# An attention and gated-MLP kernel on one core: 19 layer-norm statistics computed on ACT, k's column maxima of batches 2 to 7 by block transposes on DVE, and a new order of all steps

## The chip, the core and the metric

The kernel runs on one core of one Trainium2 chip. Its engines work side by side: PE (matrix products; PEld is its weight load), DVE (vector work), ACT (activation functions and copies), POOL (slower vector work) and SP (issues the transfers). The metric is the device time of the core in microseconds. Before the change three runs took 533.49, 533.83 and 534.16 us, a median of 533.83 us.

## What is computed

Attention with two softmaxes feeds a gated MLP whose gate mixes along the sequence. In the reference, cut to what matters (8 batches, 8 heads, 576 positions, 64 channels per head; x has 512 channels, the MLP 1024):

```python
q_s = softmax(q, axis=-1)            # over the 64 channels of a head, maximum subtracted
k_s = exp(k - np.max(k, axis=2, keepdims=True))
k_s = k_s / (np.sum(k_s, axis=2, keepdims=True) + 1e-09)     # over the 576 positions
kv = np.einsum('bhsd,bhse->bhde', k_s, v)
x = heads_joined(np.einsum('bhsd,bhde->bhse', q_s, kv))      # 8 x 576 x 512
h = gelu_tanh(x @ w_in)              # 1024 wide
u, v = h[..., :512], h[..., 512:]
v_n = (v - mean(v)) / np.sqrt(var(v) + 1e-06) * g_ln         # over the 512
v_s = np.einsum('ts,bsd->btd', w_sg, v_n) + b_sg[None, :, None]
return x + (u * v_s) @ w_out
```

## The kernel before

All of the kernel is a list of steps, the string `PLAN`. The loop at its end reads a step such as `hv_mm 3 1` and calls the function of that name with those numbers; a letter behind (`V`, `G`, `A`) names the engine of an elementwise operation that can go to several. The wrapper `InOrder` makes every engine issue its instructions in the order of `PLAN`, and matmuls are kept in that order too. Nothing reorders at run time: an instruction that waits holds all behind it on its own engine. All DVE, ACT and POOL instructions are issued on one line (L142 before), all matmuls on L330.

Precision: values that enter the large products are split into a rounded high part and a rest, and each product is three matmuls (high by high, rest by high, high by rest).

The steps of one batch b, in halves h of four heads, tiles i of 128 positions and quarters f, d, e of 128 channels:

- `load_q`, `load_k`, `load_v`: transfers on SP's queue.
- q's softmax: `q_max` (DVE), `q_swapm` (4 ACT copies of 32 rows), `q_top` (DVE), `q_sub` (POOL or DVE), `q_exp` (ACT), `q_sum` (DVE), `q_swapd` (4 ACT copies), `q_inv` (DVE), `q_mul` (POOL or DVE, twice), `q_turn` (DVE transpose, twice).
- k's softmax: `k_max` reduces five tiles to one of 128x256 in `km` by three DVE maxima. The maximum across the 128 partitions is then found by PE: `kt_mm` transposes `km` with the identity `eye` (two matmuls), `k_top` (DVE) reduces along the row to `kt`, `kb_mm` transposes `kt` back while repeating it to all partitions (two matmuls), `k_sub` (DVE, 128x1280, one operand in PSUM) subtracts it and `k_exp` (ACT) follows. `kv_mm` is 40 small matmuls; `kv_inv` and `kv_scale` (DVE) divide by the sums.
- `x_mm` gives x; `x_high` (ACT) and `x_low` (DVE) split it. `hv_mm` (12 matmuls of 512 columns) gives the v half of h, `hv_gelu` (ACT) its gelu, `hv_stat` (DVE: BN_STATS, BN_AGGREGATE and an addition of epsilon to `ve`) the statistics of a tile, `hv_pow` (POOL) the inverse root, `hv_norm` (DVE) subtracts the mean and multiplies by g_ln, `hv_high` (ACT) and `hv_low` (DVE) scale and split. The tail of 64 positions of two batches is one tile, `hv ... 4`, whose split is `tail_high`, `tail_low`, `tail_again`. That makes 36 tiles in all.
- `hu_mm` (24 matmuls of 288 columns) and `hu_gelu` give u; `sg_mm` (28 matmuls) the mixing along the sequence; `gate` (DVE) the product; `gate_high` (ACT), `gate_low` (DVE or POOL) its split; `out_mm` (24 matmuls), `out_add` (DVE), `out_rest` (DVE or POOL), `out_store` the result.
- Before that, w_in, w_out and w_sg are loaded and split once (`wi_a` to `wi_l`, `wo_a` to `wo_l`, `ws_h`, `ws_l`, `b_h`, `b_l`).

`x_mm`, `hu_mm`, `sg_mm` and `out_mm` share three PSUM buffers in turn (ps2), `hv_mm`, `kv_mm`, `kt_mm` and `kb_mm` two others (ps1). A matmul into a buffer waits until the reader of what stood in it three (or two) turns earlier is done: `hu_gelu`, `gate`, `out_add`, `x_low` for ps2, `hv_gelu`, `kv_scale`, `k_top`, `k_sub` for ps1.

## Time and profile before

| | before |
|---|---|
| median of three runs | 533.83 us (533.49 to 534.16) |
| profiled execution | 533.9 us, of which the span of the profile is 532.0 us |
| PE busy | 484.2 us (91%) in 3824 matmuls |
| DVE busy | 378.7 us (71%) in 646 instructions |
| ACT busy | 249.5 us (47%) in 425 instructions |
| POOL busy | 126.1 us (24%) in 104 instructions |
| clock granted to PE | 9 in tenths in every slice |

The profile is of one execution. Busy times are sums over the instructions of an engine; where matmuls overlap at their ends the overlap is counted once. 1.9 us of the execution lie outside the span.

### The profile page before, as it was taken

The page shows a single profiled execution, that of the slowest core. Times are in us where ns is not written, and L with a number is a line of the kernel's source. Part 1 is how long each engine was busy: PE and PEld are TensorE (multiplying, and loading weights), DVE is VectorE, ACT ScalarE, POOL GpSimd, SP SyncE. Part 2 cuts the span into 40 slices and gives each one's busy share as a digit, 9 for nine tenths or more (in the row PEclk, how much of TensorE's full clock was granted, in tenths as well). Part 3 has the DMA queues.
Part 4 walks back from the last instruction along what each step waited for, and adds up shares of the span by engine and source line. Part 5 has one row for each costly group of instructions (what it writes and reads, how often), then busy time and mean ns, then how long its engine had stood idle before and what let it go on. Part 6 is the DMA issues. An engine that isn't in the chain of part 4 may idle for free.

```text
span 532.0 us, 9264 instructions
## 1 busy us (share of the span) xinstructions
PE 484.2 (91%) x3824; PEld 444.3 (84%) x3824; DVE 378.7 (71%) x646; ACT 249.5 (47%) x425; POOL 126.1 (24%) x104
## 2 busy tenths in 40 slices
...
GB/s 322 369 388 96 17 217 81 1 46 121 168 90 38 253 91 2 44 101 68 130 39 101 111 123 90 1 101 123 67 1 1 68 23 0 1 1 68 23 1 90
DMA packets 19054, 48.87 MB, mean 92 GB/s; under 512 B 1602, under 2 KB 8132, under 8 KB 19012
## 3 DMA queue, kind: packets, MB, share of 16 engines
...
## 4 chain that ended last, share of the span: by engine, by line
PE 74%; DVE 17%; issue 3%; DMA 2%; ACT 2%; POOL 1%; SPq 0%; POOLq 0%; DVEq 0%; ACTq 0%
PE ps L330 74%; DVE km L142 2%; DVE ot_i L142 2%; DMA qq<-q 1%; DVE qm L142 1%; DVE qd L142 1%; DVE kk L142 1%; DVE v L142 1%; POOL qq L142 1%; DMA kk<-k 1%; DVE qq L142 1%; DVE s L142 1%; DVE x_l L142 1%; DVE wi_l L142 1%; DVE ulow L142 1%
## 5 line engine op out<-in xcount | busy, mean ns | idle before, releaser
L142 POOL TENSOR_TENSOR rs<-ve,half 128x1 f32<-128x1 f32 x36 | 31.0, 860 | 157.1 <-DVE ve L142 152.1
L142 DVE TENSOR_TENSOR u<-ps,u 128x576 f32<-128x576 f32 x32 | 24.0, 750 | 52.0 <-PE ps L330 52.0
L330 PE MATMUL ps<-ulow,wo_h 128*128 128x288 f32 x256 | 55.7, 296 | 1.2 <-DVE ulow L142 1.2
L330 PE MATMUL ps<-gh,wo_h 128*128 128x288 f32 x256 | 56.1, 298 | 0.5 <-ACT gh L142 0.5
L330 PE MATMUL ps<-ws_h,vnh 128*128 128x288 f32 x256 | 55.8, 299 | 0.0
L330 PE MATMUL ps<-gh,wo_l 128*128 128x288 f32 x256 | 55.3, 294 | 0.0
L330 PE MATMUL ps<-ws_l,vnh 128*128 128x288 f32 x256 | 54.8, 295 | 0.0
L330 PE MATMUL ps<-ws_h,vnl 128*128 128x288 f32 x256 | 54.8, 295 | 0.0
L142 ACT ACT_TABLE_LOAD x38 | 48.8, 1283 | 8.0 <-PE ps L330 5.1
L142 ACT ACTIVATE v<-ps 128x512 f32<-128x512 f32 x36 | 21.5, 598 | 63.8 <-PE ps L330 62.3
L142 ACT CAST gh<-u 128x576 fp32r<-128x576 f32 x32 | 21.5, 671 | 57.5 <-DVE u L142 57.3
L142 DVE TENSOR_TENSOR o<-ps,x_h 128x576 f32<-128x576 f32 (+1 forms) x33 | 24.2, 734 | 31.8 <-PE ps L330 31.8
L142 POOL TENSOR_TENSOR qq<-qq,qd 128x576 f32<-128x576 f32 x22 | 28.2, 1295 | 68.6 <-DVE qd L142 46.2
L330 PEld LDWEIGHTS ps<-gh,wo_h 128*128 128x128 f32 x256 | 41.4, 188 | 1.9 <-ACT gh L142 0.8
L142 POOL TENSOR_TENSOR ulow<-u,gh 128x576 fp32r<-128x576 f32 x16 | 23.8, 1487 | 80.7 <-ACT gh L142 62.9
L330 PEld LDWEIGHTS ps<-ulow,wo_h 128*128 128x128 f32 x256 | 41.2, 188 | 2.0 <-DVE ulow L142 1.9
L330 PEld LDWEIGHTS ps<-ws_h,vnh 128*128 128x128 f32 x256 | 41.3, 189 | 0.4
L330 PE MATMUL ps<-wi_h,x_h 128*128 128x512 f32 x144 | 40.7, 404 | 1.0 <-DVE kk L142 1.0
L330 PEld LDWEIGHTS ps<-ws_h,vnl 128*128 128x128 f32 x256 | 41.3, 188 | 0.0
L330 PEld LDWEIGHTS ps<-ws_l,vnh 128*128 128x128 f32 x256 | 41.3, 188 | 0.0
L330 PEld LDWEIGHTS ps<-gh,wo_l 128*128 128x128 f32 x256 | 41.2, 188 | 0.0
L330 PE MATMUL ps<-x_h,wi_h 128*128 128x288 f32 x256 | 40.8, 303 | 0.0
...
## 6 DMA issues: line engine op xcount, KB each, us to landing
...
```

The costliest lines, as they stand in the source:

```text
L142: ins = op(*args, **kw)
L330: tc.keep_in_program_order(nc.tensor.matmul(*args, **kw))
```

## The change

Three things are altered.

First, the statistics of 19 of the 36 tiles (0 2, 0 3, 0 4, 1 2, 2 0, 2 1, 2 4, 3 0 to 3 3, 4 2, 5 3, 6 0, 6 1, 6 3, 7 0, 7 2, 7 3) are computed on ACT. `hv_gelu` gets the letter `A` and writes the row sum beside its output; the new step `hv_sq` multiplies the sum by -1/512 (an ACT instruction on 128x1) and squares v minus the mean over 128x512 with the row sum of the squares as second output; `hv_stat ... A` is one DVE instruction on 128x1 in place of three.

Second, for batches 2 to 7 (`FOLD`) `kt_mm`, `k_top` and `kb_mm` are replaced by steps without PE: `k_fold` (DVE: a transpose of 32x32 blocks of 128x256, and a reduction to `kf`, 128x8), `k_rota` (4 ACT copies of 32x8, which move each group of 32 partitions by one), `k_maxa` (DVE, 128x8), `k_rotb` (4 ACT copies, by two), `k_maxb` (DVE: 128x8, and a block transpose that repeats the result over 128x256). `k_sub` then reads both operands from SBUF, and five of them (2 0, 4 0, 5 1, 6 1, 7 1) go to POOL.

Third, `PLAN` is written in another order from its first line to its last, the loads included, and other steps carry the letters: on DVE stand 6 instead of 8 `q_sub`, 8 instead of 10 `q_mul`, 22 instead of 16 `gate_low`, 13 instead of 20 `out_rest` and 2 instead of 4 `ws_l`; the others of these are on POOL. 50 instead of 38 loads of ACT's function tables follow from the order on ACT. The last steps, from `out_mm 7 2` on, read as before but for the quarter that each works on.

```diff
+FOLD = (2, 3, 4, 5, 6, 7)
 PLAN = """
...
-kt_mm 2 1, kb_mm 2 0, k_top 2 1, sg_mm 0 2, hv_pow 1 2, q_exp 2 0, gate 0 0, k_sub 2 0, hv_norm 1 2, gate_high 0 0, q_sum 2 0, k_exp 2 0
...
+k_maxa 3 1, q_inv 3 0, load_v 4 0, q_mul 3 0 1, q_mul 3 0 0, k_rotb 3 1, q_sum 3 1, sg_mm 1 1, hu_gelu 1 2, k_maxb 3 1, k_sub 3 1, q_swapd 3 1
+gate 1 2, k_exp 3 1, k_max 4 0, sg_mm 1 3, gate 1 1, k_fold 4 0, gate_high 1 1, q_inv 3 1, gate_high 1 2, gate_low 1 1, k_rota 4 0, kv_mm 3 1
...
+    kf_s, ka_s, kb_s = (slots(n, 2, [P, 8]) for n in ("kf", "ka", "kb"))
+    sq = sb("sq", [P, DV])
+    sm_s, nm_s, sv_s = (slots(n, 6, [P, 1]) for n in ("sm", "nm", "sv"))
...
+    def blocks(b, h, i):
+        return km_s(b, h)[:, i * 256:i * 256 + 256].rearrange("p (j c) -> p j c", c=32)
+
+    def k_fold(b, h):
+
+        m = km_s(b, h)
+        V.transpose(out=m[:, 256:512], in_=m[:, 0:256])
+        V.tensor_reduce(out=kf_s(b, h, at=h), in_=blocks(b, h, 1), axis=AX.X, op=ALU.max)
+
+    def rotate(dst, src, n):
+        for i in range(4):
+            j = (i + n) % 4
+            A.copy(out=dst[i * 32:i * 32 + 32], in_=src[j * 32:j * 32 + 32])
+
+    def k_rota(b, h):
+        rotate(ka_s(b, h, at=h), kf_s(b, h), 1)
+
+    def k_maxa(b, h):
+        V.tensor_tensor(out=kf_s(b, h), in0=kf_s(b, h), in1=ka_s(b, h), op=ALU.max)
+
+    def k_rotb(b, h):
+        rotate(kb_s(b, h, at=h), kf_s(b, h), 2)
+
+    def k_maxb(b, h):
+
+        f = kf_s(b, h)
+        V.tensor_tensor(out=f, in0=f, in1=kb_s(b, h), op=ALU.max)
+        V.transpose(out=blocks(b, h, 1), in_=f[:, :, None].broadcast_to([P, 8, 32]))
+
-    def k_sub(b, h):
+    def k_sub(b, h, E=V):
         kk = kk_s(b, h, at=h)
-        V.tensor_tensor(out=kk, in0=kk, in1=st["kb", b, h][:, None, 0:256].broadcast_to([P, 5, 256]), op=ALU.subtract)
+        top = km_s(b, h)[:, 256:512] if b in FOLD else st["kb", b, h][:, 0:256]
+        E.tensor_tensor(out=kk, in0=kk, in1=top[:, None].broadcast_to([P, 5, 256]), op=ALU.subtract)
...
+    def hv_sq(b, i):
+
+        A.mul(nm_s(b, i), sm_s(b, i), -1.0 / DV)
+        A.activation(sq, v_s(b, i), AF.Square, bias=nm_s(b, i), accum_out=sv_s(b, i))
+
+    def hv_stat(b, i, E=V):
+        if E is A:
+            V.tensor_scalar(out=ve_s(b, i), in0=sv_s(b, i), scalar1=1.0 / DV, scalar2=1e-6, op0=ALU.mult, op1=ALU.add)
+        else:
+            s6, mv = s6_s(b, i), mv_s(b, i)
+            V.bn_stats(out=s6, in_=v_s(b, i))
+            V.bn_aggr(out=mv, in_=s6)
+            V.tensor_scalar(out=ve_s(b, i), in0=mv[:, 1:2], scalar1=1e-6, scalar2=None, op0=ALU.add)
```

What stands in a row on an engine is shown at three places. In the names, `ps2_0` is the first of the three large PSUM buffers, `ps1_0` the first of the two others, and the numbers behind a name are batch and half (or quarter) and a running number.

DVE early in the program, before: the four `x_low` of batch 0 (`x_l0`) take x out of PSUM, and the second one frees the first large buffer.

```order
L142 TENSOR_TENSOR km1_0_350<-kk1_0_256 128x512
L142 TENSOR_TENSOR km1_0_350<-km1_0_350 128x256
L142 TENSOR_TENSOR km1_0_350<-km1_0_350,kk1_0_256 128x256
L142 TENSOR_TENSOR qm1_1_331<-qm1_1_331,qs1_1_342 128x36
L142 TENSOR_TENSOR wi_l_62<-ot_i_4_273,wi_h_61 128x4x128
L142 TENSOR_TENSOR wi_l_62<-ot_i_2_175,wi_h_61 128x4x128
L142 TENSOR_SCALAR ot_o_1_315<-ot_o_1_315 128x512
L142 TENSOR_TENSOR km1_1_363<-kk1_1_313 128x512
L142 TENSOR_TENSOR km1_1_363<-km1_1_363 128x256
L142 TENSOR_TENSOR km1_1_363<-km1_1_363,kk1_1_313 128x256
L142 TENSOR_SCALAR ot_i_6_361<-ot_i_6_361 128x512
L142 TENSOR_TENSOR x_l0_340<-ps2_0_73,x_h0_325 128x576
```

Between the first `x_l0` (just ahead of these rows) and the second there stand the maxima of both halves of k of batch 1 and two `wi_l`.

DVE at the same place, in the changed kernel:

```order
L148 TENSOR_REDUCE qm1_1_330<-qq1_1_195 128x36
L148 SCALAR_TENSOR_TENSOR ot_i_7_238<-raw_wo_l_87,ot_i_7_238 128x512 x2
L148 TENSOR_TENSOR km1_1_347<-kk1_1_299 128x512
L148 TENSOR_TENSOR km1_1_347<-km1_1_347 128x256
L148 TENSOR_TENSOR km1_1_347<-km1_1_347,kk1_1_299 128x256
L148 TENSOR_TENSOR x_l0_352<-ps2_0_74,x_h0_332 128x576
L148 TENSOR_TENSOR x_l0_352<-ps2_1_75,x_h0_332 128x576
L148 TENSOR_TENSOR qm1_0_319<-qm1_0_319,qs1_0_336 128x36
L148 TENSOR_TENSOR qm1_1_330<-qm1_1_330,qs1_1_342 128x36
L148 TENSOR_TENSOR km1_0_368<-kk1_0_313 128x512
L148 TENSOR_TENSOR km1_0_368<-km1_0_368 128x256
L148 TENSOR_TENSOR km1_0_368<-km1_0_368,kk1_0_313 128x256
```

The two first `x_l0` now stand together behind the maxima of one half; those of the other half and the `wi_l` come after them.

PE where the first and the second `sg_mm` of batch 0 meet, before (`vn_10`, `vn_2` and `ws_1`, `ws_2` are the tail's operands, the last two rows of an `sg_mm`):

```order
L330 MATMUL ps2_0_73<-ws_l_64,vnh_693 128x288 x2
L330 MATMUL ps2_0_73<-ws_1_65,vn_10_70 128x288 x2
L330 MATMUL ps2_0_73<-ws_2_66,vn_2_72 128x288 x2
L330 MATMUL ps1_0_76<-eye_68,km2_1_760 128x128 x2
L330 MATMUL ps1_1_77<-eye_68,kt2_0_819 128x128 x2
L330 MATMUL ps2_1_74<-ws_h_63,vnh_693 128x288 x2
L330 MATMUL ps2_1_74<-ws_h_63,vnl_694 128x288 x2
L330 MATMUL ps2_1_74<-ws_l_64,vnh_693 128x288 x2
```

Two pairs of transposes for k's maxima of batch 2 stand between the two products.

PE at the same place, in the changed kernel:

```order
L339 MATMUL ps2_0_74<-ws_l_64,vnh_636 128x288 x2
L339 MATMUL ps2_0_74<-ws_1_65,vn_10_70 128x288 x2
L339 MATMUL ps2_0_74<-ws_2_66,vn_2_72 128x288 x2
L339 MATMUL ps2_1_75<-ws_h_63,vnh_636 128x288 x2
L339 MATMUL ps2_1_75<-ws_h_63,vnl_637 128x288 x2
L339 MATMUL ps2_1_75<-ws_l_64,vnh_636 128x288 x2
```

The second `sg_mm` follows the first at once; no transpose of batches 2 to 7 is left on PE.

ACT around the last `sg_mm` steps of batch 1, before (`u1_2` and `u1_1` are written by `hu_gelu`, `gh1` by `gate_high`, `qq3`, `qq4` by `q_exp`, `qs`, `qe` by `q_swapm` and `q_swapd`):

```order
L142 ACT_TABLE_LOAD
L142 ACTIVATE u1_2_1433<-ps2_0_73 128x576
L142 CAST gh1_2_1477<-u1_2_1433 128x576
L142 ACT_TABLE_LOAD
L142 ACTIVATE qq3_1_1319<-qq3_1_1319 128x1152
L142 CAST gh1_0_1507<-u1_0_1145 128x576
L142 COPY qs4_0_1511<-qm4_0_1505 32x36 x4
L142 ACT_TABLE_LOAD
L142 ACTIVATE u1_1_1520<-ps2_0_73 128x576
L142 COPY qe3_1_1554<-qd3_1_1516 32x36 x4
L142 ACT_TABLE_LOAD
L142 ACTIVATE qq4_0_1475<-qq4_0_1475 128x1152
```

No copy for k's maxima stands on ACT here.

ACT at the same place, in the changed kernel (`ka3_1` and `kb3_1` are written by `k_rota 3 1` and `k_rotb 3 1`, `kk3_1` by `k_exp 3 1`):

```order
L148 ACT_TABLE_LOAD
L148 ACTIVATE u1_1_1479<-ps2_2_76 128x576
L148 COPY qe3_0_1485<-qd3_0_1477 32x36 x4
L148 COPY ka3_1_1514<-kf3_1_1491 32x8 x4
L148 ACT_TABLE_LOAD
L148 ACTIVATE qq3_1_1312<-qq3_1_1312 128x1152
L148 COPY kb3_1_1557<-kf3_1_1491 32x8 x4
L148 ACT_TABLE_LOAD
L148 ACTIVATE u1_2_1592<-ps2_1_75 128x576
L148 COPY qe3_1_1597<-qd3_1_1562 32x36 x4
L148 ACT_TABLE_LOAD
L148 ACTIVATE kk3_1_1436<-kk3_1_1436 128x1280
```

Between the two gelus of u stand two rounds of four copies for half 3 1, each of which a DVE maximum waits for, with a table load and the exponential of q between them.

DVE at the second of these places, in the changed kernel (`kf3_1` is k's reduced maximum, `u1_2` is written by `gate 1 2`):

```order
L148 TENSOR_TENSOR kf3_1_1491<-kf3_1_1491,ka3_1_1514 128x8
L148 SCALAR_TENSOR_TENSOR qd3_0_1477<-qd3_0_1477,qe3_0_1485 128x36
L148 RECIPROCAL qd3_0_1477<-qd3_0_1477 128x36
L148 TENSOR_REDUCE qd3_1_1562<-qq3_1_1312 128x36
L148 TENSOR_TENSOR kf3_1_1491<-kf3_1_1491,kb3_1_1557 128x8
L148 STREAM_TRANSPOSE km3_1_1481<-kf3_1_1491 128x256
L148 TENSOR_TENSOR kk3_1_1436<-kk3_1_1436,km3_1_1481 128x1280
L148 TENSOR_TENSOR u1_2_1592<-ps2_0_74,u1_2_1592 128x576
L148 TENSOR_TENSOR km4_0_1604<-kk4_0_1547 128x512
L148 TENSOR_TENSOR km4_0_1604<-km4_0_1604 128x256
```

`gate 1 2`, the row with `u1_2`, stands behind `k_maxb 3 1` and `k_sub 3 1`, which wait for the second round of copies; before, `gate 1 2` stood behind a transpose for q and ahead of `k_sub 3 1`.

## Rows read from the trace of the kernel before

**Rows 1.** The page: busy us of each engine, share of the span, instructions.

```profile
PE 484.2 (91%) x3824; PEld 444.3 (84%) x3824; DVE 378.7 (71%) x646; ACT 249.5 (47%) x425; POOL 126.1 (24%) x104
```

**Rows 2.** Four stretches: length, then busy us of each engine, clock, DMA share, GB/s.

```profile
0.00:52.00 52.00, 10.90 (x112) 7.13 (x116) 48.39 (x79) 28.36 (x56) 15.52 (x14) 1.00 0.84 300
52.00:96.00 44.00, 42.72 (x314) 35.00 (x311) 40.73 (x79) 29.83 (x51) 11.07 (x11) 1.00 0.29 95
96.00:168.00 72.00, 70.50 (x573) 67.47 (x572) 64.07 (x102) 45.81 (x80) 23.22 (x17) 1.00 0.23 79
168.00:516.00 348.00, 348.00 (x2744) 323.07 (x2745) 218.67 (x379) 144.83 (x238) 74.89 (x61) 1.00 0.18 64
```

**Rows 3.** The chain that ended last: start us, length us, engine and output.

```profile
70.21 1.40 PE ps L330 x40
...
167.85 347.34 PE ps L330 x2736
518.01 10.33 PE ps L330 x76
```

**Rows 4.** PE in order of time: start us, length us, operation, idle before and releaser.

```profile
51.75 2.18 PE L330 MATMUL ps<-qt,kvt 64*64 64x288 f32 x12 [10.96 <-DVE x_l L142]
...
96.23 0.43 PE L330 MATMUL ps<-ws_h,vnh 128*128 128x288 f32 x2
...
99.96 0.38 PE L330 MATMUL ps<-eye,km 128*128 128x128 f32 x2
100.18 0.38 PE L330 MATMUL ps<-eye,kt 128*128 128x128 f32 x2
100.31 0.51 PE L330 MATMUL ps<-ws_h,vnh 128*128 128x288 f32 x2
100.66 0.43 PE L330 MATMUL ps<-ws_h,vnl 128*128 128x288 f32 x2
100.93 0.43 PE L330 MATMUL ps<-ws_l,vnh 128*128 128x288 f32 x2
```

**Rows 5.** Groups of equal instructions: busy us, mean ns of one, idle before.

```profile
L142 DVE BATCH_NORM_STATS2 s<-v 128x6 f32<-128x512 f32 x36 | 24.8, 688 | 17.9 <-ACT v L142 17.8
L142 DVE STREAM_TRANSPOSE qt<-qq 128x576 f32<-128x576 f32 x32 | 24.4, 768 | 7.1 <-PE ps L330 3.8 <-POOL qq L142 3.0
L142 DVE TENSOR_TENSOR u<-ps,u 128x576 f32<-128x576 f32 x32 | 24.0, 750 | 52.0 <-PE ps L330 52.0
...
L142 DVE TENSOR_TENSOR kk<-kk,ps 128x1280 f32<-128x1280 f32 x16 | 23.5, 1470 | 0.0
...
L142 ACT ACTIVATE v<-ps 128x512 f32<-128x512 f32 x36 | 21.5, 598 | 63.8 <-PE ps L330 62.3 <-DVE vnl L142 1.5
...
L142 ACT ACTIVATE qq<-qq 128x1152 f32<-128x1152 f32 x16 | 18.5, 1164 | 6.0 <-DVE qq L142 3.0 <-POOL qq L142 2.9
L142 POOL TENSOR_TENSOR qq<-qq,qm 128x1152 f32<-128x1152 f32 x8 | 17.8, 2227 | 12.4 <-issue 7.3 <-DVE qm L142 4.3 <-POOL rs L142 0.7
...
L142 ACT COPY qe<-qd 32x36 f32<-32x36 f32 x64 | 14.0, 219 | 6.4 <-DVE qd L142 5.5
...
L142 DVE BATCH_NORM_AGGREGATE mv<-s 128x2 f32<-128x6 f32 x36 | 6.6, 182 | 1.2
L142 DVE TENSOR_REDUCE kt<-ps 128x2 f32<-128x256 f32 x16 | 6.5, 414 | 7.4 <-PE ps L330 7.4
```

**Rows 6.** DVE (first two) and POOL (last): start us, length us.

```profile
42.06 2.62 DVE L142 TENSOR_TENSOR km<-kk 128x512 f32<-128x512 f32 x1
...
49.09 0.68 DVE L142 TENSOR_TENSOR km<-kk 128x512 f32<-128x512 f32 x1
...
41.62 2.51 POOL L142 TENSOR_TENSOR qq<-qq,qm 128x1152 f32<-128x1152 f32 x1 [1.20 <-DVE qm L142]
```

**Rows 7.** ACT, a table load and what follows: start us, length us.

```profile
141.90 1.28 ACT L142 ACT_TABLE_LOAD   x1
143.19 1.27 ACT L142 ACTIVATE kk<-kk 128x1280 f32<-128x1280 f32 x1
```

207 lines of the change are left out of this document (105 added, 102 removed).

## The prediction

> **What bounds the kernel now.** I read the page first. It gives PE 484.2 us of work in a span of 532.0 us, DVE 378.7 and ACT 249.5 [rows 1]. Since a share over the whole span hides stages, I then read the stretches [rows 2]. They show three stages. Up to 52 us PE does about 11 us of work while DVE is busy for 48 of 52: DVE sets the pace there. From 52 to 96 us both are nearly full (42.7 and 40.7 of 44). From 96 us on PE has 70.5 of 72 us, and then 348.0 of 348: nothing but PE's own work lies on the path. The chain of waits says the same in two pieces: 347 us of matmuls in a row, and 10.33 us more that end at 518.01 + 10.33 = 528.34 us [rows 3]. The last 3.7 us of the span are an addition and a store after that. PE's granted clock is 1.00 in every stretch, the upper of the two levels, 2.4 GHz, so no term of the sum is a clock term.
>
> So a change pays in two ways only: by fewer or denser matmuls after 96 us, or by an earlier start of the first `sg_mm`, which stands at 96.23 us [rows 4]. DVE time saved after 96 us is worth nothing by itself (219 of 348 us), unless a matmul waits for it. ACT has the most room, 145 of 348 us.
>
> **The transposes that go.** Twelve halves lose `kt_mm` and `kb_mm`, a pair of matmuls each: 24 pairs. What a pair costs is read where two follow each other between two `sg_mm`: the first starts at 99.96, the second at 100.18, the next `sg_mm` at 100.31, and its second step follows after 0.35 us where the step after it takes 0.27 [rows 4]. That is 0.22 + 0.13 + 0.08 = 0.43 us for two, 0.215 us for one. One of the 24 pairs stands ahead of 96.23 us; 23 x 0.215 = 4.9 us. No other work hides them, since PE is never idle there [rows 2]. This is the firm term: **-4.9 us**, with 4.0 and 5.5 as bounds, if a pair costs 0.175 (two pairs take 0.35 us from the first's start to the next product's) or 0.24.
>
> **The work that moves, engine by engine.** DVE loses 19 BN_STATS and BN_AGGREGATE, 19 x (0.688 + 0.182) = 16.5 us, and 12 `k_top`, 12 x 0.414 = 5.0 us [rows 5]. For each fold it gets two block transposes, a reduction and two maxima of 128x8. The trace has no transpose of 128x256; the one of 128x576 takes 0.768 us [rows 5], so it lies between 0.34 (by elements) and 0.77, and I take 0.40, near the elements. With 0.41 for the reduction (the same input as `k_top`) and 0.16 for each maximum (below the 0.18 of BN_AGGREGATE, itself a small operation) a fold is 1.5 us, and 12 are 18.4. Five `k_sub` of 1.47 us go to POOL, -7.4. Net about -10 us on DVE, and a few more by the other letters.
>
> ACT gets 19 squares and multiplications. A square of 128x512 is nearest to the gelu of 128x512, 0.60 us, and a multiplication of 128x1 to a small copy, 0.22 us [rows 5]: 15.6 us, plus some if the second output costs an instruction of its own (I take nothing; 19 x 0.2 = 4 at the most). It gets 96 copies of 32x8, at most the 0.219 of those of 32x36, 20 us, and 12 table loads. The trace shows a load of 1.28 us at 141.90 and the next function's start at 143.19 [rows 7], so a load is 1.29 us: 15.5 us. Together +51, so ACT comes to about 300 us, 56% of the span. POOL gets five `k_sub` of about 2.5 us, by size from the 2.23 us of 128x1152 [rows 5].
>
> The section "What ACT_TABLE_LOAD costs" of the Trainium skill's page "ScalarE: Activation LUTs" gives 2.66 us for a switch, the load and a drain. By it the 12 loads would be 32 us, and the walk below would end 2.8 us later, a time of about 532.7 us. The row speaks against that, since the next function starts right at the load's end [rows 7].
>
> None of this is on the path by its sum. What counts is where ACT and DVE pass work back and forth while PE waits.
>
> **The start.** DVE, which sets the pace until the first `sg_mm`, has about the same work ahead of that product in both orders. The changed order lets it reach the second `x_low` of batch 0 some 5 us of DVE work sooner: one `k_max` and two `wi_l` now stand behind it. PE waits for that row today, 10.96 us until 51.75 [rows 4]. But the rows that moved behind come before the first `sg_mm` all the same, so PE will only wait later, for the `wi_l`, `k_sub 1 0` and the low part of the v tiles. I take 95.5 us for the first `sg_mm`, **-0.7 us**; from 92.5 (the sooner start is kept for the greater part) to 97.5.
>
> **New waits.** The old order's stalls after 96 us (72 - 70.5 = **1.5 us** [rows 2]) hang on steps that now stand elsewhere, so they go, and new ones come. I walked the place that looks tightest, the last `sg_mm` of batch 1. `sg_mm 1 3` needs the buffer that `gate 1 2` frees. `gate 1 2` now stands on DVE behind `k_sub 3 1`, which waits for `k_rotb 3 1` on ACT, which stands behind `q_exp 3 1`. Let 0 be the start of `sg_mm 1 2`. A product step of two matmuls takes 0.27 us [rows 4], so `sg_mm` takes 14 x 0.267 = 3.7 and `hu_mm` 12 x 0.267 = 3.2; a `kv_mm` is about 1.3 [rows 3]. PE reaches `sg_mm 1 3` at 3.7 + 1.3 + 3.2 + 3.7 = 12.0. ACT must have finished `k_exp 3 0` for the `kv_mm` at 3.7; DVE's queue lets it do so at about 3.2. After it ACT has a load (1.3), a gelu (0.6), eight copies (1.75), a load and the exponential (1.3 + 1.16): 9.3. Then on DVE `q_sum` (1.35, beside ACT's next four copies), the maximum and transpose (0.55), `k_sub` (1.47) and `gate 1 2` (0.75): 13.4. PE waits **1.4 us**, 1.9 if `k_exp 3 0` is only just in time. I take 1.6.
>
> A second such place is the v half of batch 2, where ACT does gelus, squares, two rounds of copies, eight pieces of `x_high` and two exponentials between the fourth `hv_mm` and the last. My sums come out with less than half a microsecond in hand: 0 to 2 us, I take 0.5. For the rest of the program I allow 1.0 us. New stalls: **+3.1 us**, between 0.5 and 9.
>
> Sum: 532.0 - 4.9 - 0.7 - 1.5 + 3.1 = 528.0 us span. The profiled execution took 533.9 us, 1.9 more than its span and as good as the median of 533.83. So 528.0 + 1.9 = **529.9 us**. Without the new stalls it would be 526.8; the gain is used up when they reach 7.0 us.
>
> **Rivals.**
>
> *Slower: the copies set the pace.* In-order ACT cannot let a copy for a fold pass an activation that waits. The mechanism is the one walked above; its price is 1.4 us for each fold. For it: it happens twelve times, each with two round trips from DVE to ACT, and ACT's work rises by a fifth. Against: in most places the fold has a whole batch of slack, and `k_rota` and `k_rotb` stand several steps apart. It turns the sign when five of twelve show it (5 x 1.4 + 1.5 is above 8.1). With seven, 11.3 us: 526.8 + 11.3 = **538.1 us**.
>
> *No change: POOL holds DVE.* At 42.06 a maximum of 128x512 takes 2.62 us on DVE, ends just after an operation of 2.51 us that POOL began at 41.62, and the next of its kind takes 0.68 [rows 6]. So DVE lost 1.94 us. Five `k_sub` of 2.5 us on POOL can do that five times, and `k_sub` on DVE now reads two operands from SBUF as well. If two of the five fall where PE has no slack, 2 x 1.94 = 3.9: 529.9 + 3.9 = **533.8 us**. Against: DVE has 37% of its time free after 168 us [rows 2], and only some of POOL's long operations show such a stretch in the trace.
>
> The Trainium skill, "SBUF — State Buffer", section "Who interferes with whom", says that a DVE instruction with two SBUF inputs and a GpSimd instruction that reads SBUF exclude each other for the whole instruction. By this rule, all five would hold DVE or be held, and the time would be this rival's or more. The stretch at 42.06 agrees.
>
> *More gain: the earlier start is kept.* If the later waits of the start are met in time, the first `sg_mm` comes at 92.5 us, 3.7 sooner than before, and with 2.0 us of new stalls: 532.0 - 4.9 - 3.7 - 1.5 + 2.0 + 1.9 = **525.8 us**. For it: the stretch of 1.94 us on DVE may vanish, since one of the two `q_sub` of batch 1 goes to DVE. Against: DVE's sum ahead of the product is unchanged, and DVE is busy 41 of 44 us there [rows 2].
>
> **How the numbers follow.** I give the forecast 0.52 (527 to 532.7), the earlier start 0.20, no change 0.14, slower 0.14. A difference under 0.2% (532.8 to 534.9 us) is about what a measurement of this kernel cannot tell from none. Faster: 0.52 + 0.20 = 0.72; the same 0.14; slower 0.14. The range is 525.0 to 535.5. Its lower end takes in the start at 92.5 with 1.2 us of stalls, its upper end stalls of 8.7 us. It leaves out some 0.06 below and 0.11 above.
>
> **What would show it.** In the new profile: `eye` groups of 8 instructions each in place of 32; ACT near 300 us, DVE near 365; the first `sg_mm` at 95.5 us with PE waiting on DVE before it; a wait of 1 to 2 us of PE for DVE's `u` at a `ws_h` row near 158 us, where batch 1's last `sg_mm` begins; PE otherwise dense to the end. The forecast is wrong if the first `sg_mm` lies outside 92.5 to 97.5, if copies of 32x8 take well over 0.22 us, or if PE's waits after it sum to more than 7 us.

## The result: slower by 0.34%

| | before | after |
|---|---|---|
| median us (20 runs each, side by side) | 533.79 (533.01 to 534.63) | 535.84 (533.47 to 538.18) |
| ratio after / before | | 1.0034, 95% interval 1.0022 to 1.0046 |
| profiled execution, us | 533.9 | 536.38 |
| its span, us | 532.0 | 534.6 |
| first `sg_mm` starts, us | 96.23 | 100.42 |
| last matmul ends, us | 528.33 | 530.86 |
| between these two | 432.10 | 430.44 |

The change made the kernel slower by 0.34%. The forecast was 529.9 us and faster. The table parts the miss in two: the first `sg_mm` comes 4.2 us later, where 0.7 us sooner was forecast, and what follows it takes 1.7 us less, where 3.3 less was forecast (-4.9 - 1.5 + 3.1).

### The profile after

The page of the kernel after: busy time, share of the span and instructions of each engine, the answer to [rows 1], and the granted clock in forty slices of the span.

```profile
PE 480.1 (90%) x3776; PEld 440.3 (82%) x3776; DVE 371.2 (69%) x644; ACT 303.4 (57%) x609; POOL 152.2 (28%) x116
...
PEclk9996999999999999999999999999999999999999
```

PE has 4.1 us less work than before, and ACT stands at 303 us, as forecast (300). DVE stands at 371, not 365. The amounts of work are about right. The span is not shorter.

The same stretches that [rows 2] shows, and finer, of the kernel after. Columns: stretch, length; busy time of PE, PEld, DVE, ACT and POOL; PE's granted clock (1.00 is 2.4 GHz); the transfers' share and GB/s.

```profile
52.00:80.00 28.00, 22.50 (x204) 19.10 (x200) 27.43 (x44) 25.12 (x39) 6.70 (x5) 0.94 0.14 48
80.00:96.00 16.00, 14.85 (x82) 11.09 (x79) 15.72 (x30) 11.88 (x33) 6.23 (x6) 1.00 0.44 177
...
123.00:168.00 45.00, 45.00 (x453) 43.24 (x455) 40.05 (x77) 29.71 (x66) 15.72 (x12) 1.00 0.40 142
168.00:250.00 82.00, 80.91 (x624) 71.51 (x613) 62.93 (x113) 66.55 (x137) 30.60 (x23) 0.98 0.22 80
250.00:350.00 100.00, 98.23 (x756) 90.48 (x755) 73.03 (x130) 61.02 (x124) 31.44 (x23) 1.00 0.27 96
```

From 52 to 96 us PE has 22.50 + 14.85 = 37.4 us of work, where it had 42.7 of the same 44 before: that is the late start. The clock of 0.94 there, the 6 in the page's row, is PE at the lower level up to 56 us (0.50 in 48 to 54 us, where the kernel before has 1.00). It isn't what makes PE late: the first 16 matmuls of the dense part, up to the next group's start, take 3.48 us here (52.69 to 56.17) and 3.66 in the kernel before (53.86 to 57.52, clock 1.00), and runs 1, 2 and 8 below have that clock too and start sooner or as late. Behind it PE is full, except for 82 - 80.91 = 1.1 us between 168 and 250 and 100 - 98.23 = 1.8 us between 250 and 350. In 123 to 168 us, where I had put the largest new wait (`sg_mm 1 3`), it is full, 45.00 of 45.

PE's rows of the kernel after, start and duration, operation, and in brackets the wait ahead and what ended it: the first dense product, the two longest waits from there to the first `sg_mm`, its start, and the two waits behind it with what follows the first of them. They answer to [rows 4].

```profile
52.69 2.29 PE L339 MATMUL ps<-x_h,wi_h 128*128 128x288 f32 x8
...
63.41 1.19 PE L339 MATMUL ps<-wi_h,x_h 128*128 128x512 f32 x4 [2.38 <-ACT wi_h L148]
...
68.14 0.43 PE L339 MATMUL ps<-eye,kt 128*128 128x128 f32 x2 [1.44 <-ACT v L148]
...
100.42 0.43 PE L339 MATMUL ps<-ws_h,vnh 128*128 128x288 f32 x2
...
196.71 1.98 PE L339 MATMUL ps<-qt,kvt 64*64 64x288 f32 x16 [1.00 <-DVE x_l L148]
...
200.34 1.91 PE L339 MATMUL ps<-wi_h,x_l 128*128 128x512 f32 x4
...
203.08 1.09 PE L339 MATMUL ps<-wi_h,x_h 128*128 128x512 f32 x4
...
314.85 1.19 PE L339 MATMUL ps<-wi_h,x_h 128*128 128x512 f32 x4 [1.77 <-ACT v L148]
```

The dense part begins at 52.69, 1.2 us sooner than before (53.86). Then PE waits 2.38 and 1.44 us and four times less than 1.3, and is 4.2 us late at 100.42. Before, it had no more than 44 - 42.7 = 1.3 us of idle time in the whole of 52 to 96 us. The two long waits alone don't explain the lateness: run 3 below, in the same order, has them too (2.54 and 1.44) and starts its first `sg_mm` at 95.75. There the dense part begins at 49.70, 3.0 us sooner than here, and the other 1.7 us are lost between it and the first `sg_mm`.

Its chain of waits behind the start, in columns start, length and holder, the answer to [rows 3].

```profile
180.25 3.08 DVE km L148
...
196.44 1.02 DVE x_l L148 x3
197.51 50.30 PE ps L339 x372
...
314.85 216.02 PE ps L339 x1636
```

Before, PE's piece of 347 us began at 168. Now the chain leaves PE at 180 to 197 us, for DVE's `km` of 3.08 us, ACT's work and `x_low`, and once more ahead of 314.85. The last PE piece ends at 314.85 + 216.02 = 530.87.

**Why the start is late.** DVE's rows of the kernel after, some of those ahead of 90 us; the durations are to be held against the usual one of the same form.

```profile
37.55 0.42 DVE L148 TENSOR_SCALAR ot_i<-ot_i 128x512 uint32<-128x512 uint32 x1
...
38.61 1.80 DVE L148 TENSOR_SCALAR ot_i<-ot_i 128x512 uint32<-128x512 uint32 x1
40.33 2.03 DVE L148 SCALAR_TENSOR_TENSOR ot_i<-raw_wo_l,ot_i 128x512 uint32<-128x512 uint32 x1
...
52.03 2.23 DVE L148 TENSOR_TENSOR km<-km 128x256 f32<-128x256 f32 x1
```

And POOL's rows in the same stretch.

```profile
38.58 3.23 POOL L148 TENSOR_TENSOR ws_l<-ghws,ws_h 128x640 fp32r<-128x640 f32 x2 [8.56 <-ACT ws_h L148]
...
51.36 2.62 POOL L148 TENSOR_TENSOR qq<-qq,qm 128x1152 f32<-128x1152 f32 x1 [0.20 <-DVE qm L148]
```

The pairs stand side by side. At 38.61 a shift that takes 0.42 us at 37.55 takes 1.80, and the next operation takes 2.03 where its form usually takes 0.69. POOL's two `ws_l` run from 38.58 to 41.81 beside them. At 52.03 a maximum of 0.42 us takes 2.23, beside POOL's `q_sub` of 2.62 us from 51.36. Counting each row ahead of 90 us against the usual duration of its form, DVE lost 9.5 us in nine rows (0.96, 1.06, 0.66, 0.54, 1.38, 1.34, 1.81, 1.13 and 0.66). In the kernel before it lost 3.9 there: twice 1.9, of which [rows 6] shows one.

The kernel before has a `wi_l` and a `ws_l` on POOL too, at 37.33 and 38.89. DVE's rows of before beside them show why that cost nothing.

```profile
37.98 1.33 DVE L142 TENSOR_REDUCE qm<-qq 128x36 f32<-128x1152 f32 x1
...
39.43 1.34 DVE L142 TENSOR_REDUCE qm<-qq 128x36 f32<-128x1152 f32 x1
```

DVE was at two reductions for the most part of that. Over the whole of both traces no reduction, no block transpose and no operation with an operand in PSUM takes over 0.1 us more than is usual for its form. So the same POOL instructions were free or dear by what stood beside them on DVE, and the new order put them beside operations that take all their operands from SBUF.

**Why PE waits at 196 us.** Here `k_sub 4 0` is on POOL. POOL's row and then DVE's rows there, of the kernel after.

```profile
179.78 3.26 POOL L148 TENSOR_TENSOR kk<-kk,km 128x1280 f32<-128x1280 f32 x1 [0.69 <-DVE km L148]
```

```profile
179.57 0.65 DVE L148 TENSOR_TENSOR km<-kk 128x512 f32<-128x512 f32 x1
180.25 3.07 DVE L148 TENSOR_TENSOR km<-km 128x256 f32<-128x256 f32 x1
...
183.81 0.45 DVE L148 STREAM_TRANSPOSE km<-km 128x256 f32<-128x256 f32 x1
...
195.77 1.69 DVE L148 TENSOR_TENSOR x_l<-ps,x_h 128x576 fp32r<-128x576 f32 x4 [0.57 <-ACT x_h L148]
```

DVE's maximum of 128x256 takes 3.07 us where 0.42 is usual: the second step of `k_max 4 1`, whose fold (183.81) comes late by that much. ACT, in order, waits for it, and after it has copies, two table loads, the exponential, a gelu, a square and `x_high`; DVE's `x_low` at 195.77 comes 0.57 us after DVE ran dry, and PE waits 1.00 us for it. PE then runs slower: four matmuls that take 1.09 us at 203.08 take 1.91 at 200.34. In the stretch 200 to 202 us the granted clock is 0.50, the lower level of 1.2 GHz, after 1.00 up to the wait. This is one execution: in run 1 below, with `k_sub 4 0` on POOL too, PE waits 0.99 us at the same place, keeps 1.00 and takes 4.82 us for the steps that take 203.08 - 196.71 = 6.37 here.

**And at 313 us it is POOL again.** The chain of waits of the kernel after leaves PE a last time ahead of 314.85, and it runs over DVE's `km` at 297.74. POOL's row and DVE's row there:

```profile
297.23 2.46 POOL L148 TENSOR_TENSOR qq<-qq,qm 128x1152 f32<-128x1152 f32 x1 [10.85 <-DVE qm L148]
```

```profile
297.74 2.24 DVE L148 TENSOR_TENSOR km<-km 128x256 f32<-128x256 f32 x1
```

POOL's `q_sub 6 1` holds the second step of `k_max 6 1`, 2.24 us instead of 0.42. The fold comes 1.8 us late by it, the copy of `k_rota 6 1` on ACT begins at 302.00, ACT then has 12.2 us of work in its queue up to the gelu at 314.20, and PE waits 1.77 us for that. Every profiled run of the changed order with the folds has a hold at this place (2.24 us; in run 2 the step ahead, of 128x512, takes 2.59 instead of 0.68). No run moved this `q_sub`, so what the wait would be without the hold is not shown.

### The profile page after: what moved, and what is told of

Its sections match the earlier page's. It is cut to its first block, busy times and chain, and to the rows that moved or that the text cites. A ratio compares the mean times of both kernels' runs of the same rounds, so it can differ in the third digit from the quotient of the medians.

```text
span 534.6 us, 9358 instructions
## 1 busy us (share of the span) xinstructions
PE 480.1 (90%) x3776; PEld 440.3 (82%) x3776; DVE 371.2 (69%) x644; ACT 303.4 (57%) x609; POOL 152.2 (28%) x116
## 4 chain that ended last, share of the span: by engine, by line
PE 65%; DVE 17%; DMA 8%; ACT 7%; issue 2%; SPq 1%; DVEq 0%; ACTq 0%
PE ps L339 65%; DVE km L148 4%; DMA qq<-q 3%; ACT L148 2%; DVE x_l L148 2%; DMA g_bc<-g_ln 2%; DMA raw_wo_h<-w_in 2%; DVE ot_i L148 2%; DVE o L148 1%; DVE qm L148 1%; DVE ot_o L148 1%; DVE qd L148 1%; DVE qt L148 1%; DMA kk<-k 1%; SPq L148 1%
## 5 line engine op out<-in xcount | busy, mean ns | idle before, releaser
L148 POOL TENSOR_TENSOR rs<-ve,half 128x1 f32<-128x1 f32 x36 | 29.9, 831 | 97.8 <-DVE ve L148 97.7
L148 POOL TENSOR_TENSOR qq<-qq,qd 128x576 f32<-128x576 f32 x24 | 29.9, 1258 | 76.3 <-DVE qd L148 51.5
L148 ACT ACTIVATE u<-ps 128x576 f32<-128x576 f32 x32 | 20.9, 652 | 41.1 <-PE ps L339 41.0
L339 PE MATMUL ps<-wi_h,x_l 128*128 128x512 f32 x144 | 40.8, 404 | 1.2 <-DVE x_l L148 0.9
L339 PE MATMUL ps<-x_h,wi_l 128*128 128x288 f32 x256 | 39.7, 297 | 0.0
```

The costliest lines, as they stand in the source:

```text
L148: ins = op(*args, **kw)
L339: tc.keep_in_program_order(nc.tensor.matmul(*args, **kw))
```

## Experiments

Each is compared with the kernel before, and ratios are to before. In the diffs of the order each step has a line of its own. Where nothing else is said, nothing of the computation is left out.

### 1. POOL's early subtractions taken away

`low_`, `ws_l_` and `b_l` on POOL become a fill with zeros, which reads nothing and waits for nothing; the low parts of those weights and biases are left out by this.

```diff
-            E.tensor_tensor(out=lo, in0=f32(t), in1=f32(hi), op=ALU.subtract)
+            if E is G:
+                G.memset(f32(lo), 0.0)
+            else:
+                E.tensor_tensor(out=lo, in0=f32(t), in1=f32(hi), op=ALU.subtract)
```

> The changed kernel, but the rests of w_in, w_out, w_sg and b_sg that POOL computes early (two wi_l and wo_l, three ws_l, b_l) are left out: POOL only writes zeros there, so these instructions read nothing from SBUF. In the changed kernel DVE operations beside these POOL instructions are stretched by 6.8 us in all before 90 us. Theory P (POOL's reads hold DVE and so delay the first sg_mm from 96.2 to 100.4 us): the stretches go, the first sg_mm starts at 95 to 97 us, time about 531.5 us against 535.8. Rival Q (ACT, nearly full from 55 to 98 us with its table loads, sets the pace there): the first sg_mm stays at 99.5 to 100.5, time 535 to 536 us.

Measured 532.36 us (529.23 to 533.88), ratio 0.9956 (0.9942 to 0.9970). The first `sg_mm` starts at 96.43 us, 4.0 us sooner than in the kernel after. DVE's rows of this kernel at the place shown above:

```profile
37.34 0.42 DVE L148 TENSOR_SCALAR ot_i<-ot_i 128x512 uint32<-128x512 uint32 x1
37.68 0.68 DVE L148 SCALAR_TENSOR_TENSOR ot_i<-raw_wo_l,ot_i 128x512 uint32<-128x512 uint32 x1
```

0.42 and 0.68 us, where the kernel after had 1.80 and 2.03. Of the 9.5 us that DVE loses ahead of 90 us, 6.8 stood beside the steps taken away, and the start gets 4.0 us back. So these subtractions on POOL cost the start its 4 us. The run leaves two things mixed. The low parts are there sooner for PE as well; run 8 answers that. And the fills run early (six of the nine ahead of 23 us), so few DVE operations stand beside one, and it stays open how much of this is POOL's reading and how much its mere presence. Operations with two SBUF inputs keep their length beside a fill (0.64 us at 20.43, 0.78 at 72.39); two shifts at 21.70, with one SBUF input, took 1.35 us together beside one, where one alone takes 0.42. Each of these is one or two places.

### 2. `k_sub` back on DVE

The five steps 2 0, 4 0, 5 1, 6 1 and 7 1.

```diff
-k_sub 2 0 G
+k_sub 2 0
...
-k_sub 7 1 G
+k_sub 7 1
```

> The changed kernel with the five k_sub that it gives to POOL back on DVE (+7.4 us on DVE). Theory P: the two stretches of 2.6 us on DVE at 180 and 265 us go, PE's wait for x_l at 196 us (1.0 us idle, then about 4 us at half the clock) goes with them, time 532 to 534 us. Rival Q (ACT's queue is what makes PE wait after the first sg_mm): the wait at 196 us stays, time 535.5 us or more, since DVE has more to do.

Measured 533.47 us (531.86 to 536.58), ratio 0.9997 (0.9979 to 1.0016): against the kernel after's 1.0034 this is 0.37% or 2.0 us less. The first `sg_mm` stays at 100.62 us; from there to the last matmul's end it is 427.3 us instead of 430.4. DVE's rows and PE's rows of this kernel at the place of the wait:

```profile
180.47 0.42 DVE L148 TENSOR_TENSOR km<-km 128x256 f32<-128x256 f32 x1
...
181.28 1.49 DVE L148 TENSOR_TENSOR kk<-kk,km 128x1280 f32<-128x1280 f32 x1
182.68 0.44 DVE L148 STREAM_TRANSPOSE km<-km 128x256 f32<-128x256 f32 x1
```

```profile
195.86 1.69 PE L339 MATMUL ps<-qt,kvt 64*64 64x288 f32 x16
...
200.39 1.09 PE L339 MATMUL ps<-wi_h,x_h 128*128 128x512 f32 x4
```

The subtraction takes DVE 1.49 us, and the maximum ahead of it is back at 0.42. DVE reaches its block transpose at 182.68 instead of 183.81. On POOL the step had saved DVE 1.49 us and cost it 2.65. PE's wait is gone, and its clock is 1.00 from 192 to 204 us. The `x_mm` and the product behind it take 200.39 - 195.86 = 4.53 us; the same steps of the kernel after take 203.08 - 196.71 = 6.37. So between these two executions 1.00 us of wait and 1.84 of slower matmuls make up 2.8 of the 3.1 us between 430.4 and 427.3. Most of the 1.84 is the clock, and it isn't a fixed price of the hold: run 1, with the hold and a wait of 0.99 us, takes 4.82 us for the same steps at a clock of 1.00. There the clock fell after the other wait instead (0.52 in 310 to 312 us, after 1.83 us at 309.40). The medians put the whole of moving the `k_sub` at 2.0 us.

### 3. Both at once

> Both effects at once: the early rests on POOL left out (zeros written in their place, as in e1) and the five k_sub on DVE (as in e2). If the two are separate places on PE's path, the gains add: 3.5 + 2.4 us off 535.8, 529.5 to 530.5 us, first sg_mm at 96 to 97 us and 427 us from there to the last matmul. If the second gain only filled time that the late start had opened, less: 531.5 to 532.5 us.

The edits of 1 and 2 together, so the low parts of 1 are left out here too. Measured 530.03 us (528.28 to 532.15), ratio 0.9922 (0.9902 to 0.9942). The first `sg_mm` starts at 95.75 us and 426.98 us follow. Against the kernel after: 1.0034 - 0.9922 = 1.12%, 6.0 us, and the two alone were 0.78% and 0.37%. The gains add up. With both causes away the median is what was forecast for the whole change (529.9 us, the first `sg_mm` at 95.5). That the two agree so closely is in part luck, since the hold at 313 us is still there (PE waits 1.17 us) and the low parts are left out. The profiled execution, 528.28 us, is the fastest of this kernel's runs, so its two parts are somewhat below the median's.

### 4. The statistics alone, in the order of before

The 19 tiles' statistics on ACT, each step where its DVE form stood; no folds.

```diff
-hv_gelu 0 3
+hv_gelu 0 3 A
+hv_sq 0 3
...
-hv_stat 0 3
+hv_stat 0 3 A
```

> The order of before with the statistics of the 19 tiles on ACT and nothing else. Takes 16.5 us from DVE, adds about 25 us to ACT (square 0.72, multiplication 0.2, two accumulator reads of 0.2 for each tile). If DVE's work ahead of the first sg_mm is what counts, the few tiles there make it 1 to 2 us sooner: 532 to 533.5 us. If the longer path from gelu to the normalisation (about 1.5 us on ACT and DVE in place of 1.0 on DVE) counts, PE waits: 534.5 to 537 us.

Measured 533.88 us (the lowest 533.56), ratio 0.9990 (0.9980 to 0.9999). No change that counts, between the two expectations: where PE has no gap, work taken from DVE is worth nothing.

### 5. The folds alone, in the order of before

`k_fold` and `k_rota` where `kt_mm` stood, `k_maxa` and `k_rotb` for `k_top`, `k_maxb` for `kb_mm`, batches 2 to 7.

```diff
-kt_mm 2 0
+k_fold 2 0
+k_rota 2 0
...
-k_top 2 0
+k_maxa 2 0
+k_rotb 2 0
...
-kb_mm 2 0
+k_maxb 2 0
```

> The order of before with the folds of batches 2 to 7 in place of the transposes, k_sub all on DVE: k_fold and k_rota where kt_mm stood, k_maxa and k_rotb where k_top stood, k_maxb where kb_mm stood. If 24 pairs of transposes at 0.215 us are all that matters: 533.8 - 4.9 = 528.9 us. If the copies hold ACT or the maxima hold DVE where PE waits for them: 532 to 536 us, with new PE waits for v or u in the profile.

Measured 546.95 us (546.02 to 547.74), ratio 1.0237 (1.0224 to 1.0250). PE's row with a new wait, and ACT's rows ahead of it, in this kernel:

```profile
125.88 0.73 PE L337 MATMUL ps<-gh,wo_h 128*128 128x288 f32 x2 [2.97 <-ACT gh L146]
```

```profile
104.07 0.82 ACT L146 COPY ka<-kf 32x8 f32<-32x8 f32 x4 [3.40 <-DVE kf L146]
...
123.61 0.91 ACT L146 COPY qs<-qm 32x36 f32<-32x36 f32 x4 [5.20 <-DVE qm L146]
```

ACT waits 5.20 us for DVE with a copy for q's maximum, and `gate_high` (125.18), which PE waits for, stands behind that copy in ACT's queue. That copy is not a fold's, and the kernel before has the same wait of 5.20 at 119.02, 4.6 us sooner. What is new ahead of it is the fold's copy, which holds ACT 3.40 us at 104.07, and the `q_exp` behind it starts at 107.25 instead of 101.33. PE waits 3.41 us at 174.34 in the same way, for a `gate_high` in whose queue a fold's copy waited 1.82 us at 165.44. So the rows fit the rival "the copies set the pace"; which part of the 13 us that the folds cost in this order comes from it, no run shows. The changed order has two waits of this kind, smaller ones: those at 196 and 313 us also stand behind a fold's copy that waits for `kf` (3.00 us at 184.75, 5.52 at 302.00).

### 6. No statistics on ACT, in the changed order

The 19 tiles back on DVE, the rest as after, `k_sub` on POOL included.

```diff
-hv_gelu 0 3 A
-hv_sq 0 3
+hv_gelu 0 3
...
-hv_stat 0 3 A
+hv_stat 0 3
```

> The changed kernel's order with the statistics of all 36 tiles on DVE, as before (BN_STATS, BN_AGGREGATE). DVE gets 16.5 us more, ACT loses about 36 us (19 tiles x 1.9). If the load on ACT is what makes PE wait after the first sg_mm (the gelu at 313 us, the x_high at 196 us), these waits shrink and the time falls to 532 to 534.5 us. If DVE is what PE waits for (as at the first sg_mm), the first sg_mm comes 2 us later or more and the time rises to 538 to 542 us.

Measured 535.58 us (534.84 to 536.24), ratio 1.0022 (1.0013 to 1.0030). The first `sg_mm` is 1.3 us later than in the kernel after (101.73), since DVE has the early tiles again, and the rest takes 428.3, 2.1 less. PE's rows of this kernel at the two places:

```profile
198.35 1.98 PE L337 MATMUL ps<-qt,kvt 64*64 64x288 f32 x16 [0.52 <-DVE x_l L146]
...
314.08 1.20 PE L337 MATMUL ps<-wi_h,x_h 128*128 128x512 f32 x4 [1.00 <-ACT v L146]
```

The waits are 0.52 and 1.00 us, instead of 1.00 and 1.77, and the clock stays at 1.00 behind the first of them, which is worth 6.37 - 4.83 = 1.5 us there. Together these are more than the 2.1 us. That doesn't show that the squares cause the waits: at 313 us run 3, with all squares on ACT, waits 1.17, and run 12, with none, 1.44. The median, 535.58, lies between my two expectations, and its interval overlaps that of the kernel after (1.0022 to 1.0046): what ACT's statistics are worth in this order can't be told from nothing.

### 7. No folds, in the changed order

Transposes by PE again, `k_sub` on DVE. A part of k's softmax is not the reference's here, since some `k_sub` read a PSUM buffer that has been used again.

```diff
-k_fold 2 0
-k_rota 2 0
+kt_mm 2 0
...
-k_maxa 2 0
-k_rotb 2 0
+k_top 2 0
...
-k_maxb 2 0
+kb_mm 2 0
```

> The changed kernel's order with the transposes on PE again, at the places of k_fold, k_maxa and k_maxb, and k_sub on DVE. PE gets 24 pairs, 5.2 us; ACT loses 96 copies, 20 us; POOL's k_sub, which hold DVE, are gone. If the pairs cost what the rows of before said and nothing else changes against the kernel with k_sub on DVE (533.5): 538 to 539 us. If the round trips of the folds make PE wait about as much as they save: 533 to 536 us.

Measured 545.19 us (544.89 to 545.57), ratio 1.0205 (1.0192 to 1.0219). A miss for every expectation. PE's rows with new waits in this kernel:

```profile
156.64 0.44 PE L336 MATMUL ps<-eye,km 128*128 128x128 f32 x2 [1.50 <-DVE km L145]
...
167.98 0.54 PE L336 MATMUL ps<-ws_h,vnh 128*128 128x288 f32 x2 [2.25 <-DVE u L145]
```

PE now waits for `km` ahead of its transpose (1.50 us) and for `gate` (2.25). So this isn't the price of the transposes alone: the order was made for a PE that needn't wait for `km`. Runs 5 and 7 say the same: folds and order can't be parted by one edit. What the 24 pairs alone are worth has not been measured by any run.

### 8. The early steps on DVE, with nothing left out

Run 2, and nine steps of the start go from POOL to DVE: `wi_l` 3 and 7, `ws_l` 1, 3 and 4, `wo_l` 2 and 3, `q_sub 1 0`, and `b_l` (its engine stands in its function, not in `PLAN`).

```diff
-wi_l 3
+wi_l 3 V
...
-ws_l 1
+ws_l 1 V
...
-q_sub 1 0
+q_sub 1 0 V
...
-wo_l 3
+wo_l 3 V
```

> The changed kernel with nothing left out, but the early rests of w_in, w_out, w_sg and b_sg, q_sub 1 0 and the five k_sub all on DVE: DVE gets 7.4 us for the k_sub and about 7.5 us of new work ahead of the first sg_mm and loses the stretches there, 9.5 us less the 1 us of q_mul. Theory P: the first sg_mm comes 1 us sooner, 99 to 100 us, and with the k_sub's gain the time is 531 to 533.5 us. If work on DVE there costs more than the stretches did: first sg_mm at 101 to 103 us, 534 to 537 us.

Measured 532.30 us (530.99 to 535.44), ratio 0.9970 (0.9954 to 0.9986). The first `sg_mm` comes at 98.67 us, 427.09 us follow. DVE takes on about 7.5 us of work (the estimate above) and is rid of the holds, and PE starts 2 us sooner than with `k_sub` alone moved (100.62), a little sooner than expected. So the holds cost the start also where the low parts are computed as in the reference. The time is 0.3% below the kernel before; it can't be told from run 2's with certainty (0.9979 to 1.0016 there).

### 9. The old head before the new order

The order of before up to the first `sg_mm`, the changed order behind it, `k_sub` on DVE; four tiles' statistics stay on DVE by this.

```diff
-load_q 0 1, load_q 0 0, load_k 0 1, load_eye, load_k 0 0, load_v 0 0, load_w_in 1, load_w_in 0, load_w_in 3, q_max 0 1, load_v 0 1, load_w_in 2
+load_q 0 1, load_q 0 0, load_k 0 1, load_k 0 0, load_eye, load_w_in 1, load_w_in 7, load_w_in 0, load_w_in 2, q_max 0 1, load_v 0 1, load_v 0 0
...
```

> The order of before up to the first sg_mm (with k_fold and k_maxa for batch 2's transposes, its tiles' statistics on DVE), from there the rest of the steps in the changed kernel's order, k_sub all on DVE. Theory P: the head loses only 3.9 us to POOL, the first sg_mm is back at 96 to 97 us, and the rest keeps the gain that it shows behind the first sg_mm: 529 to 531 us. If the gain behind the first sg_mm comes from work that the changed order had done ahead of it, 533 to 536 us.

Measured 535.45 us, ratio 1.0030 (1.0014 to 1.0047). The theory missed, its alternative (533 to 536 us) holds: the first `sg_mm` comes at 97.63 us, but 432.3 us follow it. PE's row of this kernel where a new wait stands:

```profile
142.26 0.54 PE L338 MATMUL ps<-ws_h,vnh 128*128 128x288 f32 x2 [2.04 <-ACT u L147]
```

A `hu_gelu` on ACT is 2.04 us late here. The order behind rests on what its own head has done by then.

### 10 to 12. Fewer tiles on ACT

All three stand on run 8. Tile `4 2`, whose square stands ahead of the late gelu at 313 us, back on DVE; then nine tiles of batches 2 to 5 (2 0, 2 1, 2 4, 3 0 to 3 3, 4 2, 5 3); then all 19.

```diff
-hv_gelu 4 2 A
+hv_gelu 4 2
...
-hv_sq 4 2
...
-hv_stat 4 2 A
+hv_stat 4 2
```

> The kernel with POOL's early rests, q_sub 1 0 and the five k_sub on DVE (532.3 us), and besides the statistics of tile 4 2 on DVE again. There PE waits 1.3 to 1.5 us for the gelu of tile 4 0 at 308 us, and ACT's queue ahead of that gelu holds tile 4 2's two accumulator reads, multiplication and square (1.3 us). If that queue sets the wait, it shrinks to under 0.4 us and the time to about 531.1 us; if the round trip of k_rotb 6 1 and q_swapd 6 1 sets it, it stays and the time is 532 to 532.5 us.

> As the last, with the statistics of all nine tiles of batches 2 to 5 on DVE again (ten tiles, of batches 0, 1, 6 and 7, stay on ACT). Taking all 19 away from ACT made the stretch behind the first sg_mm 2.1 us shorter and the start 1.3 us longer; most of the former should come from these nine. If so 530.5 to 531.5 us. If the gain there was only from less half-clock time after the wait at 196 us, which is gone already with k_sub on DVE: 532 to 533 us.

> The kernel with POOL's early rests, q_sub 1 0 and the five k_sub on DVE, and the statistics of all 36 tiles on DVE: the first part of the change is undone, the folds and the order stay. Beside the kernel with ten tiles on ACT (529.8 us) it puts 8.7 us more on DVE, five tiles of them ahead of or around the first sg_mm. If ACT's statistics of the early tiles are worth something: first sg_mm 1 us later or more, 530.8 to 532 us. If they are worth nothing: 529.3 to 530.3 us.

One tile on DVE: 531.38 us (530.33 to 531.71), ratio 0.9938 (0.9927 to 0.9950). Nine: 529.79 (529.42 to 532.53), 0.9925 (0.9907 to 0.9942). All: 532.45 (531.41 to 534.67), 0.9968 (0.9955 to 0.9981). PE's rows at the second wait, with one tile on DVE and then with nine:

```profile
310.16 1.20 PE L339 MATMUL ps<-wi_h,x_h 128*128 128x512 f32 x4 [1.20 <-ACT v L148]
```

```profile
310.42 1.19 PE L338 MATMUL ps<-wi_h,x_h 128*128 128x512 f32 x4 [1.73 <-ACT v L147]
```

In run 8 this wait is 1.32 us. It stays, with 1.20 and 1.73 us. That doesn't clear the square as a part of it: with tile `4 2` on DVE, ACT takes 11.03 us from the copy to the gelu where run 8 takes 12.20, and the copy itself comes 1.6 us later (298.48 instead of 296.90), behind a `q` that landed late: DVE waits 1.60 us for that transfer, in run 8 0.50. Neither expectation holds whole: the time fell as for a wait that goes, and the wait stayed. ACT's rows ahead of it in the kernel after:

```profile
302.00 0.81 ACT L148 COPY ka<-kf 32x8 f32<-32x8 f32 x4 [5.52 <-DVE kf L148]
...
312.91 1.28 ACT L148 ACT_TABLE_LOAD   x1
314.20 1.09 ACT L148 ACTIVATE v<-ps 128x512 f32<-128x512 f32 x2
```

In the kernel after the queue starts with the copies of `k_rota 6 1`, held up as shown above, and from then on it is full until the gelu but for 0.58 us: a gelu with its square and their second outputs, an exponential, two more rounds of copies, `x_high`, `hv_high` and three table loads; the square and its accumulator take 0.9 us of 12. With all 19 on DVE the time is that of run 8; with the ten tiles of batches 0, 1, 6 and 7 on ACT it is 0.43% lower than that (intervals of the two don't touch), and adding the nine in the middle (run 8) takes that back. Tile `4 2` alone on DVE already gives 0.9938 for run 8's 0.9970, and whether the other eight add to it isn't resolved (0.9927 to 0.9950 against 0.9907 to 0.9942). Where the gain goes the traces don't show: the three profiled executions start their first `sg_mm` at 98.67, 99.39 and 99.27 us (19, ten and no tiles on ACT) and need 427.09, 427.03 and 427.93 us from there. They are not at their medians: run 8's took 531.30 us, 1.0 below its median, the one with ten tiles 531.97, 2.2 above. The nine-tile version has the lowest median here that leaves nothing out: 0.75% below the kernel before, 1.1% below the kernel after.

## Why the prediction was wrong

- **What bounds the kernel.** Right. DVE up to the first `sg_mm`, PE behind it: run 1 takes holds from DVE ahead of it and the start gains 4 us, run 4 takes work from DVE behind it and gains nothing.
- **The transposes, -4.9 us.** Neither shown nor refuted by a run of its own. It fits: with the holds of the start and of `k_sub` gone (run 3) 426.98 us follow the first `sg_mm` instead of 432.10, which with -4.9 and -1.5 leaves 1.3 us of new waits, of which 1.17 stand in one row, at 313 us in the kernel after. The `eye` groups have 8 instructions each now, as said.
- **The start, -0.7 us: here the prediction failed.** The step was "DVE has about the same work ahead of that product in both orders". It took from equal work that DVE would reach the product at about the same time, and so that POOL would hold DVE no longer than before; no term of the sum stands for a change in that. For the work alone it was near (run 3 starts at 95.75, 95.5 was forecast). But DVE's time there is its work and the time that POOL holds it, and the second grew from 3.9 to 9.5 us: the start came at 100.42, and run 1 (96.43) and run 8 (98.67, with nothing left out) get back 4.0 and 1.8 us of it by taking POOL's instructions away. I had the mechanism in hand, [rows 6] stands in the start, and used it twice: in the rival "POOL holds DVE" for the five `k_sub`, and in "more gain" as a stretch of 1.94 us that may vanish. That the new order could bring more of them ahead of the product was in neither; the new places of the `wi_l`, `ws_l` and `wo_l` on POOL were never put beside DVE's row. Cost: 100.42 - 95.5 = 4.9 us.
- **`k_sub` on POOL, "about 2.5 us" and off the path.** Mis-sized: 3.08 us (below). The rival's price for the five, 2 x 1.94 = 3.9 us, was nearly twice what run 2 gains by the median (2.0; 3.1 in the profiled executions). Two of the five hold DVE (3.07 us each, at 180.25 and 264.96), and PE has a wait behind the first only, at 196 us. In the profiled execution over half of its price was the clock, which no term of mine had and which run 1 doesn't show at that place.
- **New waits, +3.1 us.** Measured: 430.4 - (432.1 - 4.9 - 1.5) = 4.7, if the transposes are worth their 4.9; 427.3 - 425.7 = 1.6 with `k_sub` on DVE. Of the two places named, the 1.6 us at `sg_mm 1 3` didn't come at all. The walk let ACT finish `k_exp 3 0` 3.2 us after the start of `sg_mm 1 2`; it was done after 1.3 (150.02 + 1.26 against 149.98), and `gate 1 2` after 11.8 instead of 13.4, 0.4 us before PE came to `sg_mm 1 3` at 162.16. The other, the v half of batch 2, is the place at 196 us: its 1.00 us lies in the 0 to 2 given, but with the slower matmuls that this execution has behind it, 2.8 us, it doesn't. The 1.77 us at 313, at a gelu of batch 4, are more than the 1.0 left for all the rest, and they too stand behind a hold by POOL. So the size of the sum was near and its reasons were not: both waits that came begin with a hold, which this term did not have.
- **A slip in a rival.** "The copies set the pace" turns the sign at 533.83 - 526.8 = 7.0 us, as the sum says, not at 8.1; four of twelve would do (4 x 1.4 + 1.5 = 7.1). The rival's time of 538.1 doesn't change by it.
- **Costs of ACT and DVE.** Mostly near, shown below; three terms of my sum were too small: the block transpose 0.44 (I took 0.40), the square 0.72 (0.60), and the second outputs, 3.7 + 3.5 = 7.2 us (I took nothing, 4 at the most). None of them was on the path by itself.

Groups of the kernel after by form, as in [rows 5]: name and shapes, count, then busy time and mean ns of one, then idle time ahead.

```profile
L148 POOL TENSOR_TENSOR kk<-kk,km 128x1280 f32<-128x1280 f32 x5 | 15.4, 3077 | 37.8 <-DVE km L148 29.9 <-issue 8.0
...
L148 ACT ACTIVATE sq<-v,nm 128x512 f32<-128x512 f32 x19 | 13.8, 724 | 0.6
...
L148 ACT COPY ka<-kf 32x8 f32<-32x8 f32 x48 | 9.3, 195 | 22.0 <-DVE kf L148 21.3
...
L148 DVE STREAM_TRANSPOSE km<-km 128x256 f32<-128x256 f32 x12 | 5.3, 439 | 0.1
...
L148 ACT ACTIVATION_READ_ACCUMULATOR v<-ps 128x1 f32 x19 | 3.7, 195 | 0.0
...
L148 ACT ACTIVATION_READ_ACCUMULATOR sq<-v,nm 128x1 f32 x19 | 3.5, 186 | 0.0
```

The copies take 0.195 us, below the bound of 0.219, and the square 0.72 where I took 0.60.

The sum closes: 4.9 us at the start and 4.7 - 3.1 = 1.6 behind it are 6.5; the profiled execution (536.38) lies 0.5 above the median, and 6.5 - 0.5 = 6.0 against 535.84 - 529.9 = 5.9.

The range of 525.0 to 535.5 missed by 0.3 us. Its upper end came from stalls behind the first `sg_mm`, and the start was held to 97.5 at the latest. A start at 100 was thought out nowhere.
